# A Conformer block on one core: Strassen products in two more feed-forward chunks, and the last gate blocks in two column pieces

## The chip, the cores and the metric

The kernel runs on one core of one Trainium2 chip. The metric is the device time of one execution in microseconds (us). Times before are the median of three runs; a separate execution was taken by the hardware profiler, and what is read from a trace is of that one. TensorE (PE) multiplies matrices, VectorE (DVE) and ScalarE (ACT) work on elements, GpSimd (POOL) does small things, SyncE (SP) issues DMAs.

## The reference, cut to what matters

Two sequences of 4000 tokens with 512 features go through one block, in bf16:

```python
h = _layernorm(x)
x1 = x + 0.5 * (_silu(h @ w_ff1_a) @ w_ff1_b)        # first feed-forward, 512 -> 2048 -> 512
h = _layernorm(x1)
q, k, v = h @ w_q, h @ w_k, h @ w_v
p = _softmax(jnp.einsum('btd,bsd->bts', q, k) * scale)
x2 = x1 + jnp.einsum('bts,bsd->btd', p, v) @ w_o     # attention over all 4000 tokens
h = _layernorm(x2) @ w_pw1                           # 512 -> 1024
h = h[..., :D] * _sigmoid(h[..., D:])                # the gate
dc = depthwise(h, dw)                                # 3 taps along the tokens
dc = (dc - mu) / jnp.sqrt(var + 1e-05)               # mu, var over all 8000 tokens
x3 = x2 + _silu(dc) @ w_pw2
h = _layernorm(x3)
x4 = x3 + 0.5 * (_silu(h @ w_ff2_a) @ w_ff2_b)       # second feed-forward
return _layernorm(x4)
```

## The kernel before

The 8000 tokens are 16 chunks (NCK), 8 for each sequence: 7 of 512 tokens (CHUNK) and one of 416. A chunk has four token tiles of 128. The kernel works in stages: the first feed-forward, chunk by chunk (`ff1(c)`); attention, with the convolution of earlier chunks beside it; the end of the convolution, which has to wait for the statistics of all tokens; the second feed-forward (`ff2(c)`) with the convolution's last product (`pw2`) of the chunks ahead of it. Nearly every instruction is issued through one helper, so the profile has it on line L93, and groups are told by their tiles. These are memory regions:

- `xt`: token tiles of the residual stream, and in attention forms of queries, keys and values
- `work`: layer-normalized tokens, transposed (`lnT`), small statistics, and sums of the second weight (`st.w`)
- `wff`: the feed-forward's weights (`Wa` for 512 to 2048, in 8 pieces of 256 columns; `Wb` for 2048 to 512), in the convolution `Wp1` and gate values
- `keys`: the hidden activations of a feed-forward chunk, in attention the transposed keys
- `sums`: sums for the Strassen products: of weights (`wsum`), of tokens (`lts`), and a copy of one product (`m5`)
- `s0` to `s3`, `y0` to `y3`: the eight PSUM banks (numbers 0 to 3 and 4 to 7 in the code)

**First product of a feed-forward chunk, plain.** It has 16 blocks f. A block is four matmuls of 512 columns (tokens) into one S bank (`ff_first`), then one Silu on ScalarE into `keys`.

**The same as Strassen.** Four blocks make a quad (`ff_quad`): a product of 2 x 2 halves (features in, features out) with tokens in two halves, by seven products p1 to p7 in place of eight, each of four matmuls of 256 columns. It runs in four steps on the banks 6 (y2), 3 (s3), q % 2 (s0 or s1) and 2 (s2):

- step a: p1 into y2, ScalarE copies it to h (s0 or s1); p5 into s3, ScalarE copies it to `m5`
- step b: p2 onto y2 and its Silu; p6 onto h; VectorE adds h + m5 into s2
- step c: p7 onto h; p3 onto s2 and its Silu; VectorE adds h + m5 into `m5`, and its Silu
- step d: p4 onto h and its Silu

So a quad has two ScalarE copies and two VectorE adds more than four blocks. It needs four sums of weight quarters (`wa_sums`, VectorE, once for a feed-forward; for the second they are made ahead, kept in DRAM and read back by `wa_back`) and four sums of the chunk's normalized tokens (`ln_sums`, VectorE, for each chunk). A list, `self.fast`, says which chunks run as quads: in the first feed-forward chunks 2 to 14, in the second 1 to 14. `ff_ring` says which S banks are left to other work in a chunk.

**Second product.** It is Strassen in all these chunks: units of eight matmuls of 256 columns into y0 and y1 (`ff_units`), which are issued in the next chunk at the blocks named in `ticks`; their sums of activations (`ff_sums`, `keys<-keys 128x1024`) and of weights (`ff_weights`, `work<-wff 128x2048`) are VectorE's.

**Where the second feed-forward starts.** Its chunk 0 follows the convolution's end directly: `pw1` of the last chunk (gate blocks, four matmuls over 416 columns, of which `conv_b` and `conv_a` make two for each quarter of the features), depthwise (`depthwise`, `s<-wff 128x418`), statistics, ScalarE's swishes (`work<-keys,work`), `pw2`, layer norm, transposes on TensorE, and then the first two blocks from two half-chunk products (`self.early`). In chunk 0 `pw2` of chunks 1 and 2 and the swishes of chunks 1, 2 and 3 run beside the blocks.

**What sets the order.** The program text is only a list of operations with their buffers. A planner (`Plan`) puts all of them in order on each engine: it estimates how long each takes and when a DMA has landed, lets TensorE take what is ready within 8 us of the list's order and other engines within 16 us, and runs six passes. Each engine then executes its list strictly in that order. So a changed estimate or an operation more can move instructions anywhere. For a DMA the planner's lines are these:

```python
if n.size:
    begin = max(s + (400 if n.turn else n.dur + 400), pipe)
    pipe = begin + n.size / (180 if n.turn else 260)
    n.land = pipe - s + 1000
```

Here `s` is the time of issue, `pipe` the time at which the bytes issued so far are through, and `n.turn` says that the DMA transposes.

At the very start (`head`) the tokens of chunk 0 come tile by tile; the layer norm of each tile (statistics on VectorE, a power on GpSimd, the normalization on VectorE as `work<-xt,work`), its transposes on TensorE (`y<-work 128x128`) and their copy on ScalarE (`work<-y`) are followed by the tile's 128 columns of the first four blocks (`s<-work,wff 128x128`).

Of the kernel before, what the change touches and what calls it, by code (L numbers as in the profile page):

```python
# [8 lines left out]
ALU = mybir.AluOpType  # L9
# [3 lines left out]
B, T, D, F, KW = 2, 4000, 512, 2048, 3  # L13
# [96 lines left out]
class Plan:  # L110

    PASSES = 6
    SPARE = 3000
    TABLES = {AF.Silu: 1, AF.Exp: 2, AF.Tanh: 2, AF.Sigmoid: 3, AF.Sqrt: 4}
# [158 lines left out]
    def once(self):  # L273
# [43 lines left out]
        while len(order) < len(self.nodes):  # L317
# [238 lines left out]
class Conformer:  # L556
# [35 lines left out]
    def memory(self):  # L592
# [11 lines left out]
        self.b_wsum = [E.buf("wasum", n * 4096, 4096) for n in range(4)]  # L604
# [772 lines left out]
    def wa_sums(self, w, b_w, n):  # L1377

        v = w.rearrange("p (h c) (i k f) -> p h c i k f", h=2, k=2, f=128)
        (a11, a12), (a21, a22) = [[v[:, h, :, :, k, :] for h in range(2)] for k in range(2)]  # L1380
        s1, s2, s3, s4 = self.wsum
        b1, b2, b3, b4 = [[b] for b in self.b_wsum]
        out, x, y, op, rd, wr = ((s1, a21, a22, ALU.add, [], b1), (s2, s1, a11, ALU.subtract, b1, b2),
                                 (s3, a11, a21, ALU.subtract, [], b3), (s4, a12, s2, ALU.subtract, b2, b4))[n]
        for h in range(2):
            self.S.op("DVE", lambda e, h=h: e.tensor_tensor(out=out[:, h], in0=x[:, h], in1=y[:, h], op=op),
                      reads=rd + b_w, writes=wr)
# [22 lines left out]
    def wa_back(self):  # L1410
# [6 lines left out]
                              for half in range(2)], reads=self.b_wsd, writes=self.b_wsum)  # L1417
# [13 lines left out]
    def ff_quad(self, c, q, st):  # L1431
# [9 lines left out]
                 3: (m(3), [self.b_wsum[3]], B(1, 1), right), 4: (w(1, 1), wa, T(3), [self.b_lts[s][3]]),  # L1441
                 5: (m(0), [self.b_wsum[0]], T(0), [self.b_lts[s][0]]),
                 6: (m(1), [self.b_wsum[1]], T(1), [self.b_lts[s][1]]),
                 7: (m(2), [self.b_wsum[2]], T(2), [self.b_lts[s][2]])}
# [68 lines left out]
    def ff_ring(self, c, f):  # L1513
        self.ring = [7] if self.fast[c] else [3, 6, 7] if f < 5 and c and self.fast[c - 1] else [0, 1, 2, 3]

    def ff_chunk(self, c, st, hook, done):

        fast = self.fast[c]
        own = {11: (0, 1), 12: (3,), 15: (2,)} if fast else {9: (0, 1), 10: (2, 3)}
        for f in range(FC):  # L1520
# [3 lines left out]
            if not fast:  # L1524
# [882 lines left out]
    def pw1(self, t, cb, bank=None):  # L2407
        ps, b_ps = bank or self.sbank()
        n, W = TPC if width(t) == CHUNK else TPC - 1, width(t)
        if t == NCK - 1:  # L2410
            moves = [(ps[:, 0:W], self.lin[:, :, 0:W])]
# [5 lines left out]
        for out, x in moves:  # L2417
            for cc in range(DC):
                self.mm(out, self.Wp1[:, cc, cb * 128:(cb + 1) * 128], x[:, cc], cc == 0 and out is moves[0][0], cc == DC - 1,
                        [self.b_Wp1] + self.b_lnT[1 if t == NCK - 1 else 0], b_ps, skip_group_check=True)  # L2420
# [208 lines left out]
    def program(self, any_score):  # L2629
# [50 lines left out]
        def ff1(c):  # L2680
            def hook(f):
# [7 lines left out]
                if c == 1 and f in (4, 5, 6, 7):  # L2689
                    self.wa_sums(self.Wa, self.b_Wa, (0, 1, 3, 2)[f - 4])  # L2690
# [23 lines left out]
        self.fast = [1 < c < NCK - 1 for c in range(NCK)]  # L2714
# [168 lines left out]
        heads = [self.sbank() for _ in all_t]  # L2883
        for cc in range(DC):
            self.swish(1, cc, 0)
# [77 lines left out]
        self.fast = [0 < c < NCK - 1 for c in range(NCK)]  # L2963
# [63 lines left out]
```

## Time and profile before

| what | value |
|---|---|
| median of 3 runs | 1877.64 us (1877.13 to 1879.52) |
| profiled execution | 1879.46 us |
| its span, first to last instruction | 1875.7 us |
| mean granted TensorE clock | 0.998 |
| TensorE busy | 1851.9 us, 99% |
| VectorE busy | 1465.4 us, 78% |
| ScalarE busy | 1309.2 us, 70% |
| GpSimd busy | 134.6 us, 7% |

In lines of the profile an entry gives the start in us, the duration in us, the engine, the operation, the tiles as out<-in with the shape, and a count of instructions that were merged; square brackets give the engine's idle time just before and what ended it. The printed duration of matmuls holds the time until the last result is written, and so overlaps the next one's.

### The profile page before, as it was taken

What the parts mean: (1) busy time and instruction counts of PE and PEld (TensorE: products, weight loads), DVE (VectorE), ACT (ScalarE), POOL (GpSimd) and SP (SyncE); (2) the same over time, 40 slices, a digit from 0 to 9 for tenths busy, and PEclk for the clock granted to TensorE, in tenths of its full rate; (3) what the DMA queues carried; (4) which work ended last, traced back from release to release, by engine and by line L of the source; (5) the groups of instructions that cost most, each with busy time, mean ns of one, the idle gap of its engine ahead of it and who ended that gap; (6) DMA issues with size and microseconds to landing.
All of it is one profiled execution on the core that took longest, in us unless ns stands there. A gap on an engine that the chain in (4) does not pass through costs nothing.

```text
span 1875.7 us, 39058 instructions
## 1 busy us (share of the span) xinstructions
PE 1851.9 (99%) x15271; PEld 1444.6 (77%) x15384; DVE 1465.4 (78%) x3188; ACT 1309.2 (70%) x2421; POOL 134.6 (7%) x302
## 2 busy tenths in 40 slices
PE   9999999999999999999999999999998999999998
PEld 5888888866777777777677777777774888888886
DVE  7888888868768777766777677767778888888885
ACT  5777777744666777667667677777668787777773
POOL 1000000000000000000000001000011000000000
PEclk9999999999999999999999999999999999999999
DMA  8323344197545655447954444444365222212111
GB/s 191 102 79 91 80 112 107 53 266 217 177 143 149 171 163 165 109 131 169 243 141 128 135 122 111 128 133 124 106 206 169 78 57 73 75 46 62 48 43 34
DMA packets 325014, 231.52 MB, mean 123 GB/s; under 512 B 204179, under 2 KB 295638, under 8 KB 324566
## 3 DMA queue, kind: packets, MB, share of 16 engines
q1 hardware_dynamic: 324294, 228.68, 44.6%
q8 instruction: 123, 2.02, 0.4%
q14 instruction: 69, 0.57, 0.1%
q10 hardware_dynamic: 528, 0.26, 0.0%
HBM read 128.44 MB, written 55.79 MB: 98 GB/s over the span
## 4 chain that ended last, share of the span: by engine, by line
PE 95%; ACT 2%; DVE 1%; DMA 1%; issue 1%; POOL 0%; SPq 0%; DVEq 0%; ACTq 0%
PE y L93 48%; PE s L93 47%; DVE work L93 1%; ACT work L93 1%; ACT sums L93 1%; DMA work<-work 0%; DVE xt L93 0%; DMA xt<-in_x_dram 0%; POOL work L93 0%; ACT keys L93 0%; ACT xt L93 0%; DVE s L93 0%; DVE wff L93 0%; ACT wff L93 0%; ACT s L93 0%
## 5 line engine op out<-in xcount | busy, mean ns | idle before, releaser
L93 ACT ACTIVATE sums<-s 128x512 bf16<-128x512 f32 (+2 forms) x494 | 287.0, 584 | 120.5 <-PE s L93 117.7
L93 ACT ACTIVATE keys<-s 128x512 bf16<-128x512 f32 (+2 forms) x284 | 166.3, 588 | 181.4 <-PE s L93 164.7
L93 DVE TENSOR_TENSOR sums<-sums 128x512 bf16<-128x512 bf16 (+3 forms) x528 | 195.8, 398 | 68.9 <-ACT sums L93 64.3
L93 PE MATMUL y<-work,keys 128*128 128x256 bf16 x1920 | 244.7, 273 | 0.0
L93 PE MATMUL s<-work,keys 128*128 128x256 bf16 (+5 forms) x1430 | 219.7, 290 | 1.9 <-ACT sums L93 0.4
L93 ACT ACTIVATE work<-xt,work 128x512 bf16<-128x512 bf16 x268 | 208.2, 785 | 10.3 <-DVE work L93 10.3
L93 PE MATMUL y<-sums,keys 128*128 128x256 bf16 (+1 forms) x1440 | 212.6, 270 | 0.0
L93 PE MATMUL y<-wff,keys 128*128 128x256 bf16 (+2 forms) x1590 | 208.7, 276 | 0.4 <-DVE xt L93 0.4
L93 PEld LDWEIGHTS y<-work,keys 128*128 128x128 bf16 x1920 | 187.9, 98 | 25.0
L93 PE MATMUL s<-sums 128*128 128x256 bf16 x1296 | 194.4, 273 | 0.0
L93 DVE TENSOR_TENSOR keys<-keys 128x1024 bf16<-128x1024 bf16 (+2 forms) x262 | 169.0, 663 | 28.6 <-ACT keys L93 14.8
L93 PE MATMUL y<-work,wff 128*128 128x256 bf16 (+2 forms) x1116 | 188.6, 292 | 0.0
L93 PEld LDWEIGHTS y<-wff,keys 128*128 128x128 bf16 (+1 forms) x1592 | 151.2, 98 | 32.4 <-issue 3.3
L93 DVE BATCH_NORM_STATS2 work<-xt 128x6 f32<-128x512 bf16 x251 | 164.1, 681 | 5.0 <-DMA xt<-in_x_dram 4.2
L93 PEld LDWEIGHTS s<-work,keys 128*128 128x128 bf16 (+1 forms) x1456 | 118.2, 97 | 56.8 <-ACT sums L93 5.1
L93 PEld LDWEIGHTS y<-sums,keys 128*128 128x128 bf16 x1440 | 137.1, 98 | 27.1 <-issue 6.1
L93 POOL TENSOR_TENSOR work<-work 128x4 f32<-128x4 f32 (+3 forms) x107 | 91.0, 851 | 804.2 <-DVE work L93 801.7
L93 PE MATMUL y<-sums,xt 128*128 128x256 bf16 (+1 forms) x960 | 145.6, 270 | 0.0
L93 PE MATMUL s<-work,wff 128*128 128x512 bf16 (+5 forms) x668 | 141.8, 347 | 2.8 <-DVE work L93 2.7
L93 PEld LDWEIGHTS s<-sums 128*128 128x128 bf16 x1296 | 126.7, 98 | 20.0
L93 PE MATMUL s<-work 128*128 128x512 bf16 (+4 forms) x513 | 122.9, 374 | 5.8 <-DVE work L93 1.4
L93 PE MATMUL s<-xt,keys 128*128 128x256 bf16 (+1 forms) x816 | 124.3, 270 | 2.6 <-DVE xt L93 2.3
(143 smaller groups left out, 3182.6 us busy)
## 6 DMA issues: line engine op xcount, KB each, us to landing
xt<-kfd SPq DMA_DIRECT2D x98, 384.0 KB, 3.3
xt<-v12d SPq DMA_DIRECT2D x105, 256.0 KB, 2.8
xd<-xt SPq DMA_DIRECT2D x28, 512.0 KB, 3.0
xt<-xd SPq DMA_DIRECT2D x28, 512.0 KB, 4.6
out_dram<-xt SPq DMA_DIRECT2D x14, 512.0 KB, 3.0
xt<-in_x_dram SPq DMA_DIRECT2D x13, 512.0 KB, 4.0
dcvd<-wff SPq DMA_DIRECT2D x48, 128.0 KB, 2.1
keys<-dcvd SPq DMA_DIRECT2D x12, 512.0 KB, 4.0
```

Of the source, the lines that this page charges most:

```text
L93: return getattr(eng, self.name)(*self.args, **self.kw)
```

## The change

It has five parts.

1. `self.fast` of the first feed-forward begins with chunk 1 instead of 2. The weight sums, until now made in chunk 1 at f = 4 to 7, are made in chunk 0 at f = 8 to 15, in two halves by output features (`part`), with a buffer for each half, so that a half needs four of the eight weight pieces.
2. `self.fast` of the second feed-forward begins with chunk 0, and `self.mixed` is set: chunk 0 has its blocks 0 to 3 plain, and blocks 4 to 15 as three quads. Its token sums are made at f = 0 and 1. For its first four blocks `ff_ring` takes the S banks in an order (`self.turn`) that continues the one of the convolution's end. Its first unit of the second product is no longer issued at the end of chunk 0.
3. `pw1` of the last chunk has the first two of the four `a` and of the four `b` blocks in two column pieces, 256 and 160: the first piece reads token tiles 0 and 1 alone.
4. The planner takes a transposing DMA that stands behind bytes of others to land 1500 ns later (`BEHIND`).
5. The half-chunk products of `self.early` clear their bank once for both halves.

```diff
+    BEHIND = 1500
...
             if n.size:
                 begin = max(s + (400 if n.turn else n.dur + 400), pipe)
+                behind = self.BEHIND if n.turn and pipe > s + 400 else 0
                 pipe = begin + n.size / (180 if n.turn else 260)
-                n.land = pipe - s + 1000
+                n.land = pipe - s + 1000 + behind
...
-    def wa_sums(self, w, b_w, n):
-
-        v = w.rearrange("p (h c) (i k f) -> p h c i k f", h=2, k=2, f=128)
+    def wa_sums(self, w, b_w, n, part):
+
+        at = slice(part * HF // 2, (part + 1) * HF // 2)
+        v = w.rearrange("p (h c) (i k f) -> p h c i k f", h=2, k=2, f=128)[:, :, :, at]
...
+        rd = b_w[part * len(b_w) // 2:(part + 1) * len(b_w) // 2]
...
     def ff_ring(self, c, f):
-        self.ring = [7] if self.fast[c] else [3, 6, 7] if f < 5 and c and self.fast[c - 1] else [0, 1, 2, 3]
+        if c == 0 and self.mixed and f == 2:
+            self.rings["S"] = 0
+        self.ring = (self.turn if self.mixed else [0, 1, 2, 3]) if c == 0 and f < 4 else [7] if self.fast[c] else [3, 6, 7] if f < 5 and c and self.fast[c - 1] else [0, 1, 2, 3]
...
-            if not fast:
+            if not fast or mixed and q == 0:
                 self.ff_block(c, f, st)
             elif r == 0:
                 quad = self.ff_quad(c, q, st)
...
+            if mixed and f < 2:
+                self.ln_sums(c, f)
...
     def pw1(self, t, cb, bank=None):
         ps, b_ps = bank or self.sbank()
+        first = cb % DC < 2
...
         if t == NCK - 1:
-            moves = [(ps[:, 0:W], self.lin[:, :, 0:W])]
+            b_x, cut = self.b_lnT[1], [0, 2 * TILE, W] if first else [0, W]
+            moves = [(ps[:, lo:hi], self.lin[:, :, lo:hi]) for lo, hi in zip(cut, cut[1:])]
...
-        for out, x in moves:
+        for n, (out, x) in enumerate(moves):
+            rd = b_x[2 * n:2 * n + 2] if t == NCK - 1 and first else b_x
...
-                if c == 1 and f in (4, 5, 6, 7):
-                    self.wa_sums(self.Wa, self.b_Wa, (0, 1, 3, 2)[f - 4])
+                if c == 0 and f >= 8:
+                    self.wa_sums(self.Wa, self.b_Wa, (0, 1, 3, 2)[f % 4], (f - 8) // 4)
...
-        self.fast = [1 < c < NCK - 1 for c in range(NCK)]
+        self.fast = [0 < c < NCK - 1 for c in range(NCK)]
+        self.mixed = False
...
+        self.turn = [self.b_S.index(b) for _, b in heads[2:] + heads[:2]]
...
-                            cc == 0, cc == DC - 1, [self.b_Wa[f * self.NWA // FC]] + self.b_lnT[0][2 * h:2 * h + 2], b_ps)
+                            cc == 0 and h == 0, cc == DC - 1, [self.b_Wa[f * self.NWA // FC]] + self.b_lnT[0][2 * h:2 * h + 2],
+                            b_ps, skip_group_check=True)
...
-        self.fast = [0 < c < NCK - 1 for c in range(NCK)]
+        self.fast, self.mixed = [c < NCK - 1 for c in range(NCK)], True
```

More of the change, by code (lines that the diff above doesn't have):

```diff
@@ L603, in memory @@
         self.wsum = [E.view(n * 4096, 2048).rearrange("p (c i f) -> p c i f", c=2, i=HF) for n in range(4)]
-        self.b_wsum = [E.buf("wasum", n * 4096, 4096) for n in range(4)]
+        self.b_wsum = [[E.bufs("wasum", [(n * 4096 + c * 2048 + k * 1024, 1024) for c in range(2)]) for k in range(2)]
+                       for n in range(4)]
         self.lts = [[E.view(16384 + s * 4096 + n * 1024, 512).rearrange("p (t c k) -> p t c k", t=2, c=2)
@@ L1416, in wa_back @@
                                                                self.wsd[half].rearrange("p (m f) -> p m f", m=8))
-                              for half in range(2)], reads=self.b_wsd, writes=self.b_wsum)
+                              for half in range(2)], reads=self.b_wsd, writes=sum(self.b_wsum, []))
     def ln_sums(self, c, step):
@@ L2416, in pw1 @@
                 moves.append((ps[:, n * TILE:W], self.lnT[0][:, n, :, tile_rows(t, n)]))
[L2417 removed]
+        for n, (out, x) in enumerate(moves):
+            rd = b_x[2 * n:2 * n + 2] if t == NCK - 1 and first else b_x
             for cc in range(DC):
[L2419 to L2420 removed]
+                self.mm(out, self.Wp1[:, cc, cb * 128:(cb + 1) * 128], x[:, cc], cc == 0 and n == 0, cc == DC - 1,
+                        [self.b_Wp1] + rd, b_ps, skip_group_check=True)
         return ps, b_ps
```

21 lines of the change are left out of this document (11 added, 10 removed).

## The prediction

> **What bounds the kernel now.** I read the page first: the span, the busy shares and the chain that ended last.
>
> ```profile
> span 1875.7 us, 39058 instructions
> PE 1851.9 (99%) x15271; PEld 1444.6 (77%) x15384; DVE 1465.4 (78%) x3188; ACT 1309.2 (70%) x2421; POOL 134.6 (7%) x302
> PE 95%; ACT 2%; DVE 1%; DMA 1%; issue 1%; POOL 0%; SPq 0%; DVEq 0%; ACTq 0%
> ```
>
> TensorE (PE) is busy for 99% of the span and carries 95% of the chain. So a change can act in two ways only: fewer columns through TensorE, or another length of the few stalls between them. The profiled execution took 1879.46 us, 3.76 more than its span; the median of the three runs is 1877.64. I work out a difference from the trace and take it off that median; off the profiled time it would give a figure 1.8 higher.
>
> The order of the instructions of the changed program shows where they went; it gives no time. TensorE has 100 matmuls more: 12 for each of seven quads (four in the first feed-forward's chunk 1, three in the second's chunk 0) and 16 for the split gate blocks. There are 14 more ScalarE copies and 14 more VectorE adds of quads, 8 more token sums on VectorE, and no more DMAs.
>
> **1. Columns saved.** The timeline of TensorE gives the price of a matmul as it is paid in a full queue, which is the distance of starts and not the printed duration (that holds the pipeline's tail).
>
> ```profile
> 200.33 1.91 PE L93 MATMUL y<-work,keys 128*128 128x256 bf16 x16
> ...
> 209.93 0.60 PE L93 MATMUL s<-sums 128*128 128x256 bf16 x4
> ...
> 1436.17 3.62 PE L93 MATMUL s<-work,wff 128*128 128x512 bf16 x16
> 1439.62 1.03 PE L93 MATMUL s<-work 128*128 128x512 bf16 x4
> ```
>
> Between the first two rows 88 matmuls of 256 columns start in 9.60 us: 0.109 each. Sixteen of 512 columns take 3.45 us: 0.2156 each. Four plain blocks are sixteen of the latter, 3.45 us; a quad is 28 of the former, 3.06. That saves 0.395, and 2.77 us for seven. The split of four gate blocks adds 16 instructions and no columns; two of 256 cost 0.218 against 0.2156 for one of 512, so 0.003 each, 0.04 together. Both lie on TensorE, which is the path.
>
> **2. The head of the kernel.** The weight sums of the first feed-forward now run on VectorE in chunk 0. Nobody needs them soon, but the planner puts four of them (512 elements each) ahead of the normalization of token tile 3, and the first of the four waits for the DMAs of weight pieces 0 to 3. VectorE works in order, so that normalization waits too, and behind it TensorE's transposes of tile 3, ScalarE's copy of them, and the last column piece of the first four blocks.
>
> ```profile
> 2.59 3.83 SPq L93 DMA_DIRECT2D wff<-in_w_ff_a_dram  x5
> wff<-in_w_ff_a_dram SPq DMA_DIRECT2D x5, 256.0 KB, 5.6
> 9.05 0.41 DVE L93 TENSOR_SCALAR work<-xt,work 128x512 bf16<-128x512 bf16 x1 [0.52 <-POOL work L93]
> 12.44 2.47 DVE L93 BATCH_NORM_STATS2 work<-xt 128x6 f32<-128x512 bf16 x4 [2.98 <-DMA xt<-in_x_dram]
> 47.23 0.76 DVE L93 TENSOR_TENSOR sums<-work 128x512 bf16<-128x512 bf16 x2 [0.95 <-DMA work<-work]
> 47.91 0.88 DVE L93 TENSOR_TENSOR sums<-work,sums 128x512 bf16<-128x512 bf16 x2
> 9.91 0.39 PE L93 MATMUL y<-work 128*128 128x128 bf16 x4
> 10.32 10.00 PE L93 MATMUL s<-work,wff 128*128 128x128 bf16 x68
> 11.65 3.26 ACT L93 ACTIVATE keys<-s 128x512 bf16<-128x512 f32 x6 [0.71 <-PE s L93]
> ```
>
> Piece 3 is the third of SyncE's five issues, at about 3.6 to 4.1, and lands a median 5.6 later: 9.2 to 9.7, take 9.3 (the tokens of chunk 1, behind it in the queue, are there by 12.44). The four sums at 0.38 to 0.44 each end at 10.9, the normalization at 11.3 instead of 9.46. The transposes then start at 11.35 instead of 9.91, and take 0.4 to their end; the copy takes 0.6, so 12.35. Four matmuls of 128 columns and their tail (0.4) close the first block, and its Silu starts at 12.75 instead of 11.65: 1.1 late. The fifth block needs the bank that this Silu empties, and from there on TensorE had no gap in which to catch up. I take **+1.0**; the bounds are 0.3 (the weights are there by 8.5) and 1.5.
>
> Further on, VectorE is full in just the stretch that has to make the token sums for chunk 1's first quads:
>
> ```profile
> 20.00:44.00 24.00, 23.89 (x158) 14.83 (x159) 23.18 (x41) 14.56 (x28) 1.40 (x1) 1.00 0.62 139
> ```
>
> (Columns: length, busy PE, weight load, VectorE, ScalarE, GpSimd, clock, DMA.) Following VectorE's new order with these durations from 16.5 on, the token sums of tiles end at 23.9 and 25.4, while TensorE reaches the products that need them at 25.9 and 27.7; the first quad's add ends at 29.2, its user comes at 30.7. So no stall, with 1.5 to 2 us in hand; if that cover is gone it costs what the four quads saved, 1.6.
>
> **3. Gate blocks of the last chunk in two pieces.** The timeline before the convolution's last chunk:
>
> ```profile
> 1406.37 0.39 PE L93 MATMUL y<-work 128*128 128x128 bf16 x4
> 1407.79 0.86 PE L93 MATMUL s<-work,wff 128*128 128x416 bf16 x4 [1.04 <-DVE work L93]
> ...
> 1417.17 0.69 PE L93 MATMUL s<-wff 128*128 128x418 bf16 x3
> 1417.91 0.38 PE L93 MATMUL y<-work 128*128 128x512 bf16 x1
> ```
>
> TensorE ends its transposes at 1406.6 (four of 0.056) and begins the first gate block at 1407.79, when the copies of token tiles 2 and 3 are done: 1.2 us empty. The new order has twelve matmuls of 256 columns there, from three blocks, that need tiles 0 and 1 alone: 1.31 us of work that fits the hole. From 1407.79 to 1417.9 TensorE ran without a gap, so what comes earlier stays earlier, unless VectorE, at work almost without a break on the convolution's statistics, holds it. **−1.1**, bounds −1.25 and 0.
>
> **4. Second feed-forward, chunk 0.** Its 22 us:
>
> ```profile
> 1427.60:1449.60 22.00, 20.83 (x103) 10.56 (x106) 18.73 (x34) 19.28 (x33) 1.88 (x1) 0.92 0.55 156
> 1439.10 1.88 POOL L93 TENSOR_TENSOR work<-work 128x4 f32<-128x4 f32 x1 [12.07 <-DVE work L93]
> 1445.46 0.81 PE L93 MATMUL s<-work 128*128 128x512 bf16 x3 [0.50 <-ACT keys L93]
> L93 ACT ACTIVATE s<-y 128x512 f32<-128x512 f32 x56 | 32.9, 588 | 0.6
> L93 ACT ACTIVATE work<-keys,work 128x512 bf16<-128x512 bf16 x40 | 31.6, 812 | 8.1 <-PE y L93 7.8 <-PE s L93 0.3
> L93 DVE TENSOR_TENSOR s<-s,sums 128x512 f32<-128x512 f32 x56 | 38.8, 694 | 2.8 <-PE s L93 2.3 <-ACT keys L93 0.3 <-ACT xt L93 0.3
> ```
>
> Three quads bring 6 copies of 0.59 to ScalarE (3.5 us), 6 adds of 0.69 and 4 token sums of 0.4 to VectorE (5.7). ScalarE has 2.7 free and VectorE 3.3, so some work has to move out: the swishes (0.81 each) and the feed-forward's own sums can go on into chunk 1, and TensorE gets second-matmul units of chunk 0 as filling. Along the new order TensorE is 0.5 to 1 us behind ScalarE at each bank. At one place VectorE is late: the shift behind GpSimd's 1.88 us power is now ahead of a 1.2 us weight sum and of the second quad's add, and TensorE, which wants that add, waits 1.0. Against that the 0.50 wait at 1445.46 goes. Net **+0.5**; bounds −0.6 and, if nothing moves out, +3.
>
> **5. Transposes behind other DMAs.** The planner now takes a DMA transpose queued behind another transfer to land 1.5 us later. The place:
>
> ```profile
> 835.66 2.75 SPq L93 DMA_TRANSPOSE work<-work  x2
> 841.85 0.42 ACT L93 ACTIVATE work<-work 128x256 bf16<-128x256 bf16 x1 [3.46 <-DMA work<-work]
> 841.86 0.60 PE L93 MATMUL y<-sums,keys 128*128 128x256 bf16 x4
> 844.30 0.53 PE L93 MATMUL s<-xt,keys 128*128 128x208 bf16 x4 [1.84 <-DVE xt L93]
> ```
>
> ScalarE stands 3.46 us at transposes, VectorE's reciprocal behind ScalarE, and TensorE loses 1.84. In the new order ScalarE's instructions at this place are the same, but the transposes go ahead of one 1.2 us transpose of keys and one of the casts before them is ScalarE's. I take **−0.7**, between 0 and −2.0, nearer to the half because the queue of the same engine stays. Other neighbours moved by a place or two along all of attention, where waits on DMAs are far shorter.
>
> **Sum.** −2.77 + 0.04 + 1.0 − 1.1 + 0.5 − 0.7 = −3.0 us: 1877.64 becomes **1874.6** (a span of 1872.7). That is −0.16%, within the 0.2% (3.75 us) that a measurement of this kernel can tell from no change.
>
> **The clock.** Around the second feed-forward's start the granted clock falls:
>
> ```profile
> 1426.00:1430.00 4.00, 2.56 (x20) 1.94 (x20) 3.37 (x11) 3.36 (x7) 0.70 (x1) 0.78 1.09 357
> 1430.00:1432.00 2.00, 1.62 (x9) 1.21 (x10) 1.90 (x4) 1.74 (x3) 0.00 (x0) 0.59 1.07 378
> ```
>
> Together these make about 3.4 us at half clock. I leave the term at zero, since the same sparse stretch is in the new order; bounds are −0.8 (it goes) and +1.7 (a second one of full matmul work, half of 3.4). [...]
>
> **Rivals.**
> - *Both waits close* (18%). The transposes land before ScalarE needs them (−2.0 instead of −0.7), and chunk 0 covers its hand-offs and loses its old wait (−0.6 instead of +0.5): −5.4, 1872.2. For it: the transposes have one queue place less ahead. Against: ScalarE's order is unchanged there.
> - *A second slow stretch of the clock* (10%), if the second feed-forward's quads leave TensorE with more short gaps: −3.0 + 1.7 = −1.3, 1876.3.
> - *VectorE becomes the bound in the first feed-forward* (8%), 23.18 of 24 us being full: the four quads' 1.6 is not kept: −1.4, 1876.2.
> - *Slower: the three quads run in series* (8%). A quad is four hand-offs: 4 × 0.44 of products, two of 0.59 to ScalarE, two of 0.69 to VectorE and four tails of 0.16, 5.0 us. With one 0.81 swish ahead at each of ScalarE's two, 6.6, or 3.5 over the 3.06 of its own matmuls, 10.6 for three; the convolution's twenty matmuls of 512 columns cover 4.3 of it at most, some 3 since they wait for VectorE too. Then +7.6 stands in place of +0.5: +4.1, 1881.7. It decides where ScalarE's queue is over 1 us late at the first quad's copy. For it: 19.28 of 22 us busy. Against: along the new order the copies come in time.
>
> **The numbers.** The forecast has 56%, with a range of its own of 1873.0 to 1876.2. Faster by over 0.2% is a third of it and the first rival, 36%; slower by over 0.2% is three quarters of the last, 6%; within, 58%. The range leaves out the last rival and the ends of the first: 1871.8 to 1878.2.
>
> **What would show it.** Right: 28 matmuls of 256 columns in place of 16 of 512 for each quad, at 0.109; the first Silu at about 12.7; the gap before the last chunk's first gate block under 0.2; one wait of about 1 us on VectorE in the second feed-forward's chunk 0; the wait at 844 about halved. Wrong: a Silu at 11.7, ScalarE waits of over 2 us in the quads, a wait on VectorE between 25 and 45, or new waits in attention.

## The result, and the profile after

The changed kernel takes 1875.51 us (median of 22 executions, 1873.52 to 1877.11), the kernel before 1878.69 (22 executions beside it, 1876.68 to 1880.54). The ratio is 0.9982 with a 95% interval of 0.9976 to 0.9988: 3.2 us or 0.17% faster, where 3.0 was forecast. The profiled execution took 1876.08 us.

From the page of the changed kernel, the span, the busy line and the chain:

```profile
span 1871.9 us, 39333 instructions
PE 1851.6 (99%) x15370; PEld 1453.3 (78%) x15484; DVE 1471.1 (79%) x3212; ACT 1317.5 (70%) x2441; POOL 135.4 (7%) x302
PE 93%; DVE 2%; ACT 2%; DMA 1%; issue 1%; SPq 1%; DVEq 0%
```

Busy time is no measure of what changed (1851.6 against 1851.9): a printed duration runs on past the next start (3.62 us for sixteen matmuls of 512 columns whose starts take 3.45), and there are 99 matmuls more. What counts is when the same instruction starts. In a part of the program where both orders issue the same things, the difference of the starts says how far the changed kernel is ahead by then. The timeline of TensorE gives these anchors, after:

```profile
199.64 1.91 PE L93 MATMUL y<-work,keys 128*128 128x256 bf16 x16
...
842.41 0.60 PE L93 MATMUL y<-sums,keys 128*128 128x256 bf16 x4
842.85 0.52 PE L93 MATMUL s<-xt,keys 128*128 128x208 bf16 x4
...
1403.93 0.39 PE L93 MATMUL y<-work 128*128 128x128 bf16 x4
1404.15 1.75 PE L93 MATMUL s<-work,wff 128*128 128x256 bf16 x16
...
1422.05 0.40 PE L93 MATMUL s<-work 128*128 128x128 bf16 x4 [1.25 <-ACT work L93]
...
1485.50 0.60 PE L93 MATMUL s<-sums,wff 128*128 128x256 bf16 x4
```

and two rows of before beside those that the prediction shows:

```profile
1425.57 0.40 PE L93 MATMUL s<-work 128*128 128x128 bf16 x4 [1.25 <-ACT work L93]
...
1488.85 0.60 PE L93 MATMUL s<-sums,wff 128*128 128x256 bf16 x4
```

| stretch | before | after | ahead | gained in the stretch | forecast |
|---|---|---|---|---|---|
| head and first feed-forward (`y<-work,keys` x16) | 200.33 | 199.64 | 0.69 | 0.7 | 0.6 (1.6 columns, -1.0 head) |
| attention (by 1350 us) | | | 2.32 | 1.6 | 0.7 |
| to the second feed-forward's transposes (`s<-work` 128x128) | 1425.57 | 1422.05 | 3.52 | 1.2 | 1.1 |
| second feed-forward, chunk 0 and start of 1 (`s<-sums,wff`) | 1488.85 | 1485.50 | 3.35 | -0.2 | 0.7 (1.2 columns, -0.5 waits) |

The figure at 1350 us is the median over matmuls of the same tiles. So two parts came out near the forecast, and two did not: attention gained 0.9 more, the second feed-forward 0.9 less. These two misses cancel. TensorE's last matmul ends 3.2 earlier; the spans differ by 3.7, the last 0.5 of it in what follows that matmul, which nothing in the change touches.

The head, in the timeline after:

```profile
9.00 1.10 DVE L93 TENSOR_TENSOR sums<-wff 128x512 bf16<-128x512 bf16 x3 [0.75 <-DMA wff<-in_w_ff_a_dram]
...
10.47 0.41 DVE L93 TENSOR_SCALAR work<-xt,work 128x512 bf16<-128x512 bf16 x1
...
11.12 0.39 PE L93 MATMUL y<-work 128*128 128x128 bf16 x4
...
12.63 3.19 ACT L93 ACTIVATE keys<-s 128x512 bf16<-128x512 f32 x6 [0.49 <-PE s L93]
```

The first sums wait for the weights until 9.00, the normalization of tile 3 comes behind four of them at 10.47, its transposes at 11.12, the first Silu at 12.63 instead of 11.65. That is the chain of the prediction, link by link.

VectorE's window in the first feed-forward (length, PE, weight load, VectorE, ScalarE, GpSimd, clock, DMA) did not become a bound:

```profile
20.00:44.00 24.00, 23.89 (x195) 18.46 (x196) 22.46 (x45) 16.09 (x32) 1.09 (x1) 1.00 0.62 151
```

### The profile page after: what moved, and what is told of

Read it like the earlier page. It is cut to its first block, busy times and chain, and to the rows that moved or that the text cites. A ratio compares the mean times of both kernels' runs of the same rounds, so it can differ in the third digit from the quotient of the medians.

```text
span 1871.9 us, 39333 instructions
## 1 busy us (share of the span) xinstructions
PE 1851.6 (99%) x15370; PEld 1453.3 (78%) x15484; DVE 1471.1 (79%) x3212; ACT 1317.5 (70%) x2441; POOL 135.4 (7%) x302
## 4 chain that ended last, share of the span: by engine, by line
PE 93%; DVE 2%; ACT 2%; DMA 1%; issue 1%; SPq 1%; DVEq 0%
PE y L93 48%; PE s L93 45%; ACT sums L93 1%; DVE work L93 1%; DVE xt L93 1%; SPq L93 1%; ACT work L93 0%; DMA kfd<-xt 0%; DVE sums L93 0%; DMA vhd<-wff 0%; DVE wff L93 0%; ACT wff L93 0%; ACT keys L93 0%; DMA wff<-keysd 0%; DMA work<-work 0%
## 5 line engine op out<-in xcount | busy, mean ns | idle before, releaser
L93 ACT ACTIVATE sums<-s 128x512 bf16<-128x512 f32 (+3 forms) x501 | 290.4, 584 | 112.2 <-PE s L93 108.4
L93 ACT ACTIVATE keys<-s 128x512 bf16<-128x512 f32 (+2 forms) x271 | 158.7, 588 | 176.0 <-PE s L93 158.1
L93 PE MATMUL s<-sums 128*128 128x256 bf16 x1380 | 206.1, 273 | 0.8 <-DVE sums L93 0.6
L93 PE MATMUL y<-work,wff 128*128 128x256 bf16 (+3 forms) x1168 | 196.1, 291 | 0.0
L93 PEld LDWEIGHTS s<-sums 128*128 128x128 bf16 x1380 | 134.6, 98 | 23.9 <-DVE sums L93 0.8
L93 PEld LDWEIGHTS y<-work,wff 128*128 128x128 bf16 x1168 | 113.0, 98 | 25.8 <-ACT s L93 0.4
L93 PE MATMUL s<-work 128*128 128x512 bf16 (+5 forms) x494 | 118.7, 376 | 5.3 <-DVE work L93 1.4
```

What stands on the lines that cost most here:

```text
L93: return getattr(eng, self.name)(*self.args, **self.kw)
```

## The experiments

All start from the changed kernel unless said otherwise, and each was timed in 11 executions beside 33 of the kernel before. They came in three groups, with medians of the kernel before of 1878.65 (n_behind0 to n_pw1), 1879.84 (the next four in the table) and 1878.83 (the last four), so the ratios are to be compared rather than the medians. The last four columns give, for the profiled execution, how far the kernel is ahead of the one before at four places (300 us; 1350 us; the first transposes of the second feed-forward; 1530 us), all from the timeline of TensorE.

| kernel | edit | median, us | ratio to before (95%) | 300 | 1350 | transposes | 1530 |
|---|---|---|---|---|---|---|---|
| changed kernel | | 1875.51 | 0.9982 (0.9976 to 0.9988) | 0.68 | 2.32 | 3.52 | 3.35 |
| n_behind0 | planner's term 0 | 1874.78 | 0.9979 (0.9970 to 0.9988) | 0.59 | 2.25 | 2.90 | 4.15 |
| n_ff1 | first feed-forward as before | 1876.55 | 0.9990 (0.9981 to 0.9999) | -0.14 | 1.51 | 2.14 | 3.13 |
| n_ff2 | second's chunk 0 plain | 1875.89 | 0.9983 (0.9974 to 0.9992) | -0.97 | 0.85 | 2.05 | 2.05 |
| n_pw1 | gate blocks whole | 1877.95 | 0.9994 (0.9985 to 1.0003) | -0.13 | 1.94 | 1.65 | 3.43 |
| p_pw1 | kernel before, gate blocks split | 1877.53 | 0.9987 (0.9978 to 0.9996) | 0.06 | 0.43 | 1.89 | 1.83 |
| e_wsum | weight sums after all pieces | 1877.72 | 0.9989 (0.9980 to 0.9998) | -0.59 | 2.16 | 3.02 | 2.11 |
| e_wsum_b0 | the same, planner's term 0 | 1879.61 | 1.0000 (0.9991 to 1.0009) | -2.41 | -0.72 | 0.64 | 0.14 |
| e_2quads | two quads, not three | 1876.78 | 0.9984 (0.9975 to 0.9993) | 0.42 | 1.93 | 3.13 | 3.78 |
| h5 | weight sums behind tile 3 | 1875.58 | 0.9983 (0.9974 to 0.9992) | 0.96 | 2.69 | 4.13 | 3.34 |
| l1 | earlier layer norm of chunk 1 | 1878.48 | 0.9996 (0.9987 to 1.0005) | 0.39 | 1.99 | 3.19 | 3.18 |
| h5l1 | both | 1875.81 | 0.9983 (0.9974 to 0.9992) | 1.06 | 2.44 | 3.88 | 3.93 |
| h5l1b0 | both, planner's term 0 | 1878.28 | 0.9997 (0.9988 to 1.0006) | 0.84 | 2.27 | 3.55 | 2.36 |

An interval is some 3.4 us wide, as much as the whole effect. So the medians tell little about a single part; the places in the traces tell more, though one execution still differs from the next. One such difference has a name: a stretch of half clock at the start of the second feed-forward, worth 1.24 us (last section), stands in the profiled executions of the kernel before, the changed kernel, n_ff2, p_pw1, e_wsum, h5 and h5l1b0, and in none of the other seven. In the last column those seven are ahead by about 1.24 for the clock alone, an estimate from one pair of traces.

A gap of TensorE is here the distance of two starts less what the first matmul takes in a full queue (0.056 us for 128 columns, 0.109 for 256, 0.2156 for 512); the idle time that a row prints in brackets is some 0.16 shorter, because the printed duration runs on by as much (3.62 us where the starts take 3.45).

**The planner's term for transposes, and attention.** Two kernels undo one possible cause each.

```diff
 n_behind0:
-    BEHIND = 1500
+    BEHIND = 0
```

> The changed kernel with the planner's term for transposes set back to 0; all else stays. Theory A (the term itself shortens attention, by what the two traces differ between 425 and 1400 us, 1.6): the time goes up by 1.6 against the changed kernel, to 1.5 below the kernel before, and TensorE's wait near 844 us (1.84 in the kernel before) is back. The prediction's size of the same theory: up by 0.7. Theory B (any replanning moves attention's short waits by chance, the term has no effect of its own): the wait near 844 need not come back, others appear elsewhere, and the change against the changed kernel is anywhere between -1.5 and +1.5.

```diff
 n_ff1:
-        self.fast = [0 < c < NCK - 1 for c in range(NCK)]
+        self.fast = [1 < c < NCK - 1 for c in range(NCK)]
...
-                if c == 0 and f >= 8:
-                    self.wa_sums(self.Wa, self.b_Wa, (0, 1, 3, 2)[f % 4], (f - 8) // 4)
+                if c == 1 and f in (4, 5, 6, 7):
+                    for part in range(2):
+                        self.wa_sums(self.Wa, self.b_Wa, (0, 1, 3, 2)[f - 4], part)
```

> The changed kernel with the first feed-forward as it was: chunk 1 in plain blocks, the weight sums in chunk 1 at f = 4 to 7. Theory A: at 300 us this kernel is 0.68 behind the changed one (1.58 of columns come back, 0.90 of the head goes), the first Silu starts at 11.65 in place of 12.63, and attention, which keeps the planner's term, stays 1.6 shorter than before. Theory B: attention's order is planned anew here too, so its length differs from the changed kernel's by up to 1.5 either way. Rival for the head: if tile 3's tokens and not the weight sums made the first Silu late, it stays near 12.6 and 1.58 is lost in full.

With the term at 0 the wait near 844 us stayed away. The timeline of TensorE in n_behind0, at the place where the kernel before waits 1.84:

```profile
841.31 0.60 PE L93 MATMUL y<-sums,keys 128*128 128x256 bf16 x4
841.75 0.52 PE L93 MATMUL s<-xt,keys 128*128 128x208 bf16 x4
```

Between 300 and 1350 us n_behind0 gains 1.66 and n_ff1 1.65, the changed kernel 1.64. So the term is not needed for what attention gained; nor are the quads of chunk 1. Nor did the time of n_behind0 go up by 0.7 or 1.6 as theory A has it: its median is 0.7 below the changed kernel's. A third kernel shows that the wait belongs to the old order and is no accident of one execution:

```diff
 p_pw1: the kernel before, with the function pw1 of the changed kernel
```

> The kernel before with the column pieces of the last chunk's gate blocks alone; its order in attention is that of the kernel before, instruction for instruction. Theory: the wait near 844 us follows from that order, so it is there again with 1.5 to 2 us, and attention is as long as before; the hole ahead of the first gate block is gone, and the time is 1.1 below the kernel before. Rival: the wait near 844 was one execution's late transfer; then it is missing here, and this profiled span is some 3 below the one of before.

Its order in attention is that of the kernel before, and the wait is back in the timeline:

```profile
838.42 2.42 SPq L93 DMA_TRANSPOSE keys<-keysd  x1
...
841.76 0.42 ACT L93 ACTIVATE work<-work 128x256 bf16<-128x256 bf16 x1 [3.42 <-DMA work<-work]
...
844.22 0.53 PE L93 MATMUL s<-xt,keys 128*128 128x208 bf16 x4 [1.79 <-DVE xt L93]
```

Against that the changed kernel, whose order here leaves two transposes and a follower of half the length:

```profile
835.70 2.51 SPq L93 DMA_TRANSPOSE work<-work  x2
838.25 1.27 SPq L93 DMA_TRANSPOSE keys<-keysd  x1
...
839.52 0.42 ACT L93 ACTIVATE work<-work 128x256 bf16<-128x256 bf16 x1 [0.58 <-DMA work<-work]
```

ScalarE waits 3.42 in the one and 0.58 in the other, though the transposes of `work` start at nearly the same time (835.66 in the kernel before, 835.70 here). What differs in the queue is the transpose of `keys` behind them, 2.42 against 1.27, and that another one of `keys` goes ahead of them in the old order (834.32 in the kernel before). That order of the four transposes does not decide it alone: e_wsum and e_wsum_b0 have the same four in the same order, with 1.25 and 1.28 for the last, and there ScalarE waits 2.05 and 1.67 and TensorE not at all. Why the DMAs took longer in the old order was not tried. All twelve kernels whose order in attention is another gain 1.4 to 2.8 between 300 and 1350 us, three of them with the term at 0 (1.66, 1.69, 1.43). They have seven different orders between them: n_ff2, n_pw1, e_2quads and l1 have that of the changed kernel, and h5l1 that of h5. p_pw1, with the order of the kernel before, gains 0.37. So theory A, and with it the prediction's cause, falls as far as the term is not needed: the old order had one bad place, and each new one that was tried passes it. Theory B's statement that the term has no effect of its own fits this but is not shown, since the term alone was not put into the kernel before; its expectation that gains and losses are evenly spread did not come true.

New waits came too, and they follow from the order in part: the gap after 602 us is 0.34 in the changed kernel, 0.64 in n_ff2, 0.45 in n_pw1 and 0.62 in l1, all four with the same order there; the one after 591 is 0.50, 0.26, below 0.24 and 0.40. In the changed kernel a transfer stands ahead of both: ScalarE waits 1.94 us for `work<-work` until 589.04, and VectorE 1.07 for `wff<-keysd` until 600.39. Whether their landing makes the sizes differ was not tried.

**The head.** n_ff1, without weight sums in chunk 0, has its first Silu at 11.79: its rival is out. Its length at 300 us, -0.14, is as expected (0.68 behind was expected against the changed kernel, 0.82 came). The delay is larger than 1.0 in other executions of the same order. VectorE's wait and the first Silu in n_pw1:

```profile
9.95 1.10 DVE L93 TENSOR_TENSOR sums<-wff 128x512 bf16<-128x512 bf16 x3 [0.76 <-DMA wff<-in_w_ff_a_dram]
...
13.40 3.19 ACT L93 ACTIVATE keys<-s 128x512 bf16<-128x512 f32 x6 [0.49 <-PE s L93]
```

The first sums start at 9.00, 9.49, 9.95, 9.44 and 9.46 in the five kernels with this order (changed, n_ff2, n_pw1, e_2quads, l1), and the first Silu at 12.63, 12.95, 13.40, 12.89 and 12.92: the head costs 1.0 to 1.75 by when the weights land.

```diff
 e_wsum:
-        rd = b_w[part * len(b_w) // 2:(part + 1) * len(b_w) // 2]
+        rd = b_w
```

> The changed kernel with both halves of the weight sums of the first feed-forward reading all eight weight pieces, so that none of them can stand ahead of token tile 3's normalization. Theory (the head's delay is VectorE waiting for the first weight pieces, 1.0 to 1.75 by how late these land in an execution): the first Silu starts at 11.6 to 11.8, and at 300 us the kernel is 1.58 ahead of the kernel before; the time is 1.0 to 1.7 below the changed kernel's. Rival: VectorE, 22.5 of 24 us busy between 20 and 44 us, now has some 2.8 us more of sums there, the token sums and adds of chunk 1's quads come late, and TensorE loses between 25 and 45 us what the head gains: no change.

The head came back in full (chunk 1's transposes start within 0.02 of the kernel before), and yet at 300 us the kernel is 0.59 behind instead of 1.58 ahead. The windows of VectorE and the waits of TensorE in e_wsum:

```profile
20.00:44.00 24.00, 23.90 (x196) 18.55 (x197) 23.80 (x51) 16.43 (x32) 1.09 (x1) 1.00 0.62 154
44.00:68.00 24.00, 22.57 (x190) 17.70 (x190) 19.82 (x47) 19.50 (x36) 2.02 (x2) 1.00 0.38 84
```

```profile
56.28 0.81 ACT L93 ACTIVATE work<-xt,work 128x512 bf16<-128x512 bf16 x1 [1.63 <-DVE work L93]
...
61.03 0.61 PE L93 MATMUL y<-work,wff 128*128 128x256 bf16 x4 [0.66 <-ACT keys L93]
...
67.06 1.05 PE L93 MATMUL y<-wff,keys 128*128 128x256 bf16 x8 [0.32 <-DVE keys L93]
```

VectorE is busy for 23.80 of 24 us, where the changed kernel has 22.46, and TensorE for 22.57 of 24 in the stretch after it, with four gaps (0.42, 0.31, 0.82, 0.49). The first row shows the way: ScalarE stands 1.63 for what VectorE has to make before a chunk can be normalized, and then has these normalizations between the Silus that TensorE waits for. The rival is right, some 20 us later than it said. So the early weight sums pay about 1 us at the head to save 2 between 53 and 67 us, and the prediction's third rival (VectorE as the bound) is real and close: with 1.3 us more of VectorE work in those 24 us it came true.

```diff
 e_wsum_b0: as e_wsum, and BEHIND = 0
```

> As e_wsum, and the planner's term for transposes is 0. If what shortened attention is any new order and not the term, the wait near 844 us stays away here too, attention is 1.5 to 2 shorter than before, and the second feed-forward begins without a slow stretch of the clock as it did with the term at 0 alone: 5 to 5.5 below the kernel before, the fastest so far. If the orders differ by chance, between 3 and 5 below.

The wait near 844 stayed away, and attention gained 1.69, as the first half says. The rest missed: 0.2 below the kernel before, not 5. It has the waits of e_wsum, one single gap of 1.28 at 165.5 us that its neighbours lack (the same kind stands in n_ff2 at 164 us, with 1.32, where VectorE waited 2.22 for transposed tokens), and gaps of 2.09 and 0.86 at the start of the second feed-forward's chunk 1. There the first token sum starts 3.2 us after the row of the four DMA transposes ends (1445.33 and 1448.52), in the changed kernel 1.3 (1444.89 and 1446.22); why they land so late was not tried.

```diff
 h5:
-        rd = b_w[part * len(b_w) // 2:(part + 1) * len(b_w) // 2]
+        rd = b_w[part * len(b_w) // 2:5 if part == 0 else len(b_w)]
```

> The changed kernel with the first half of the weight sums reading five weight pieces in place of four. The planner then puts the normalization of token tile 3 ahead of them and keeps them early, so VectorE does not carry them into the stretch from 45 to 68 us as in e_wsum. Theory (the loss at the head is that one normalization standing behind the sums; the loss in e_wsum was VectorE's load after it): first Silu at 11.7 to 11.9, no new waits up to 100 us, at 300 us 1.4 to 1.6 ahead of the kernel before where the changed kernel was 0.68; time 0.9 to 1.6 below the changed kernel's. Rival: the sums, now later by a piece, hold chunk 1's statistics and norms, and a wait of 0.5 or more appears between 20 and 70 us: half the gain or none.

The timeline of h5:

```profile
9.45 0.41 DVE L93 TENSOR_SCALAR work<-xt,work 128x512 bf16<-128x512 bf16 x1 [0.74 <-POOL work L93]
11.25 1.43 DVE L93 TENSOR_TENSOR sums<-wff 128x512 bf16<-128x512 bf16 x4 [1.38 <-DMA wff<-in_w_ff_a_dram]
...
12.24 3.26 ACT L93 ACTIVATE keys<-s 128x512 bf16<-128x512 f32 x6 [0.49 <-PE s L93]
```

The normalization of tile 3 is ahead of the sums now (9.45), no new wait appears up to 100 us, and the first Silu starts at 12.24. That is half of the way: the planner also moved the transposes behind more of the first blocks. At 300 us h5 is 0.96 ahead, h5l1 1.06; the five executions of the changed kernel's order had 0.68, -0.13, 0.42, 0.39 and 0.36 (n_ff2, before its single gap), 0.34 in the mean. So 0.6 to 0.7 is gained at the head, where 0.9 to 1.6 was expected; the median, 1875.58, is that of the changed kernel.

**The gate blocks in two pieces.**

```diff
 n_pw1:
-        first = cb % DC < 2
+        first = False
```

> The changed kernel with all gate blocks of the last chunk in one column piece. Theory: the hole of 1.2 us between the transposes of the last chunk's tokens and its first gate block is back, the stretch from there to the second feed-forward is 1.08 longer, and the time 1.1 longer than the changed kernel's, 2.1 below the kernel before. Rival: VectorE's statistics set the end of that stretch anyway, so only part, 0 to 0.5, is lost. The waits near 591 and 844 us are as in the changed kernel if they follow from the order.

The timelines, without the pieces (n_pw1) and with them (p_pw1):

```profile
1404.72 0.39 PE L93 MATMUL y<-work 128*128 128x128 bf16 x4
1406.15 0.86 PE L93 MATMUL s<-work,wff 128*128 128x416 bf16 x4 [1.04 <-DVE work L93]
```

```profile
1405.56 0.39 PE L93 MATMUL y<-work 128*128 128x128 bf16 x4
1405.79 1.75 PE L93 MATMUL s<-work,wff 128*128 128x256 bf16 x16
```

The hole of 1.2 us is back in the one and gone in the other. From 1350 us to the transposes p_pw1 gains 1.46 on the kernel before, and n_pw1 loses 0.29 where the changed kernel gains 1.20: 1.5 by both, more than the hole, because gaps of 0.41 and 0.29 among the transposes ahead of it went with it. By the ratios the pieces are worth 0.12% (n_pw1) and 0.13% (p_pw1), 2.3 to 2.4 us; the rival is out, the rest above 1.5 lies within the intervals.

**Second feed-forward, chunk 0.**

```diff
 n_ff2:
-        self.fast, self.mixed = [c < NCK - 1 for c in range(NCK)], True
+        self.fast, self.mixed = [0 < c < NCK - 1 for c in range(NCK)], False
```

> The changed kernel with the second feed-forward's chunk 0 in plain blocks throughout; the order of everything ahead of it is the same. By the trace of the changed kernel the three quads save 1.19 in columns and bring about 1.3 of new waits (copies, VectorE's adds, VectorE at the transposes of chunk 1's tokens): between 0.3 faster and 0.2 slower than the changed kernel. By the prediction's size (0.5 of waits): 0.7 slower. The wait near 591 us (0.5) is there and the one near 844 is not, if these follow from the order of the instructions; if they are chance of one execution, they differ.

It is 0.4 slower than the changed kernel by the medians, between the two expectations and closer than the intervals can tell. By the traces it neither gains nor loses from the transposes to 1530 us (2.05 and 2.05), where the changed kernel loses 0.17. The waits that ate the columns are these in the changed kernel:

```profile
1434.38 0.61 PE L93 MATMUL s<-sums 128*128 128x256 bf16 x4 [0.19 <-ACT sums L93]
...
1446.70 1.22 PE L93 MATMUL s<-sums 128*128 128x256 bf16 x8 [0.56 <-DVE sums L93]
...
1446.22 0.43 DVE L93 TENSOR_TENSOR sums<-work 128x512 bf16<-128x512 bf16 x1 [1.45 <-DMA work<-work]
...
1438.95 5.94 SPq L93 DMA_TRANSPOSE work<-work  x4
```

The first (a gap of 0.35) is a copy of ScalarE that comes late; one of 0.26 follows at 1439; the largest, 0.72, is the first quad of chunk 1, whose token sums wait for four DMA transposes in series (1438.95 to 1444.89, landed by 1446.2). VectorE stands for 1.45 there.

```diff
 e_2quads:
-            if not fast or mixed and q == 0:
+            if not fast or mixed and q < 2:
...
-        self.ring = (self.turn if self.mixed else [0, 1, 2, 3]) if c == 0 and f < 4 else [7] if self.fast[c] else ...
+        self.ring = (self.turn if self.mixed else [0, 1, 2, 3]) if c == 0 and f < 8 else [7] if self.fast[c] else ...
```

> The changed kernel with two quads in place of three in the second feed-forward's chunk 0 (blocks 0 to 7 plain). If each quad keeps its 0.395 and the waits there come from the number of hand-offs, one quad less costs 0.4 of columns and takes a third or more of the 1.36 of waits away: between 0.1 slower and 0.5 faster than the changed kernel. If the waits come from VectorE standing at chunk 1's transposes, they stay, and it is 0.4 slower.

With one quad less the wait at chunk 1's transposes shrank to 0.27, but others came (gaps of 0.39, 0.45 and 0.60):

```profile
1432.15 2.76 PE L93 MATMUL s<-work,wff 128*128 128x512 bf16 x12 [0.22 <-DVE xt L93]
...
1436.94 1.05 PE L93 MATMUL y<-work,keys 128*128 128x256 bf16 x8 [0.29 <-DVE keys L93]
...
1448.08 0.81 PE L93 MATMUL y<-work 128*128 128x512 bf16 x3 [0.44 <-DVE xt L93]
```

Its ratio, 0.9984, is that of the changed kernel within the interval. What it gains in this stretch, 0.65, is less than the clock alone makes (1.24, last section). So the waits come neither from the number of quads alone nor from the transposes alone.

```diff
 l1:
-                if c == 0 and f in (2, 4):
-                    ti = 1 + f // 2
+                if c == 0 and f in (1, 2):
+                    ti = 1 + f
...
-                        self.ln_job(1, "in", "ACT", (3, 4, 5, 7, 7, 8, 8, 8, 9, 9))
+                        self.ln_job(1, "in", "ACT", (2, 3, 3, 4, 4, 4, 5, 5, 5, 5))
```

> The changed kernel with the convolution's last product for tiles 2 and 3 of chunk 1 at f = 1 and 2 in place of 2 and 4, and chunk 1's layer norm listed 1 to 4 blocks earlier, in the second feed-forward's chunk 0. Theory (the wait of 0.7 to 2 at the start of chunk 1 is the chain residual, statistics, norm, four transposes in series, token sum; it is late because the quads brought TensorE forward): the transposes end some 2 us earlier than in the changed kernel, that wait goes, and the kernel is 0.5 to 0.8 below the changed one. Rival: ScalarE, 20.0 of 22 us busy there, is the limit; then the copies of the quads come later by the swishes that the earlier product needs, waits of the same size appear inside chunk 0, and the time stays.

The window of 22 us in l1, and its timeline:

```profile
1424.09:1446.09 22.00, 20.11 (x147) 13.44 (x148) 21.83 (x45) 21.52 (x37) 1.01 (x1) 1.00 0.59 170
```

```profile
1433.95 0.60 PE L93 MATMUL y<-work,wff 128*128 128x256 bf16 x4 [0.34 <-ACT keys L93]
...
1440.78 1.04 PE L93 MATMUL y<-work 128*128 128x512 bf16 x4 [0.42 <-DVE xt L93]
...
1447.33 0.61 PE L93 MATMUL s<-sums 128*128 128x256 bf16 x4 [0.35 <-DVE s L93]
...
1436.94 5.14 SPq L93 DMA_TRANSPOSE work<-work  x4
```

The transposes end 2.8 earlier (1442.08 against 1444.89), as planned. But VectorE is busy for 21.83 of 22 us and ScalarE for 21.52 (19.30 and 20.02 in the changed kernel's same window), and the waits are now at ScalarE's and VectorE's hand-offs inside the chunk; the one at chunk 1's start (a gap of 0.52) is VectorE's add. The time stays, as the rival said: both engines are full, and what is moved forward pushes something else back. Being full is not enough for a wait, though: n_pw1 has 21.27 and 21.65 of 22 us there (from 1426 us) and is the best of all, with waits of 0.39 and 0.28 only. Over all kernels with three quads, this stretch (transposes to 1530 us) gains between -1.2 and -0.2 where the clock is slow and between -0.5 and 1.8 where it is not. With the 1.24 (from one pair of traces) taken off the latter, eight of these ten traces lose time here against the kernel before, up to 1.7, and the best gains 0.5, where n_ff2 without any quad has 0.00. So the traces do not show that the three quads pay; the 0.4 by which the median of n_ff2 is slower lies within the intervals. The waits of the quads are a matter of the order, and none of the edits tried commands them.

```diff
 h5l1: the edits of h5 and l1;  h5l1b0: and BEHIND = 0
```

> Both edits, of h5 and of l1. If they are independent, the sum of the two: 1.4 to 2.4 below the changed kernel, 4.6 to 5.6 below the kernel before.

> As h5l1, with the planner's term for transposes at 0. If the term does nothing of its own for attention, the wait near 844 us stays away, attention is 1.5 to 2 shorter than in the kernel before, and the time is within 0.7 of h5l1. If it does, this kernel is 1.6 above h5l1.

h5l1 is as fast as the changed kernel and no faster: h5's 0.6 is there, l1's gain is not. In h5l1b0 the wait near 844 stays away and attention is as short (1.43 against 1.38), as expected of a term without effect there; but its time, 2.5 above h5l1, misses the 0.7. In the trace it falls back behind the second feed-forward's transposes (3.55 down to 2.36), but these 1.2 are as much as the half clock made in the one pair of traces (1.24), and it stands in this execution and not in that of h5l1. So the trace does not explain the medians' 2.5, and what does is open. No run beat the changed kernel beyond its interval; n_behind0, with the term at 0, is as fast.

## Why the prediction was right, and where it was not

The sum was right, -3.0 forecast and -3.2 measured, in part because two errors of 0.9 cancelled.

1. *Columns saved* (-2.77). At 300 us the changed kernel is 0.68 ahead after losing 0.90 at the head (chunk 1's transposes start at 21.06, before at 20.16): 1.58, which is four times 0.395. For the three quads of the second feed-forward it can't be separated from their waits.
2. *The head* (+1.0). Mechanism and chain as described. In the profiled execution 0.90; over five executions of this order the first Silu is 1.0 to 1.75 late, above the bound of 1.5 in one. The step that was too low is the landing of the weights (9.3 taken; the sums began at 9.0 to 9.95). The cover that VectorE was to have in chunk 1 held, and e_wsum, with 1.3 us more of VectorE's work from 20 to 44 us, shows that there was not much more of it.
3. *Gate blocks in two pieces* (-1.1, bounds -1.25 and 0). The hole is gone as described. The stretch gained 1.5, outside the bound: the gaps among the transposes ahead of the hole were not counted.
4. *Second feed-forward, chunk 0* (+0.5, bounds -0.6 and +3). This term was mis-sized: from the transposes to 1530 us the kernel lost 0.17 where the columns save 1.19, so waits cost 1.36 more than before. (The gaps account for 1.1 of it: 0.35, 0.26 and 0.72, some 0.45 in gaps of 0.03 to 0.16 at hand-offs, less the old 0.66; the rest is in no single gap.) The place named, VectorE's add behind GpSimd's power and a weight sum, is there, but with 0.26 and not 1.0. The old wait at 1445.46 went. What was missing is the start of chunk 1, 0.72, whose tokens' transposes are no longer hidden when TensorE arrives 1.2 us sooner, and ScalarE's late copy, 0.35. The prediction looked at the hand-offs of the quads and not at what the next chunk needs in time. With the columns of term 1 the three quads were to gain 0.7; at the same clock only n_pw1's trace shows a gain (0.5).
5. *Transposes behind other DMAs* (-0.7, between 0 and -2.0). The wait went altogether (842.41 and 842.85 follow without a break), and attention gained 1.6, new waits of 0.84 at 591 and 602 included, which were among the prediction's signs of being wrong. The forecast was half of what came, and the cause was wrong in that the term is not needed: with it at 0 the same happens. That this term of the sum had the right sign is luck.
6. *The clock* (0). One stretch before, one after, each of 3.4 us at half clock; right for these two executions. That the sparse stretch brings the slow one was the author's estimate: e_2quads has the same idle times there and stays at 1.00.

Of the rivals, the first (both waits close) was half true: the wait at 844 closed, the hand-offs did not. VectorE as the bound of the first feed-forward was one edit away. A second slow stretch and the quads in series did not come: no ScalarE wait in the quads is over 2 us.

## What to carry to other kernels

Where an order is planned, a changed estimate or an operation more gives a new order everywhere; before a gain far from the edit is put down to the edit, undo the edit and see whether the gain goes. Work taken off the critical engine brings forward the time at which the next stage's inputs are due: the longest serial chain into that stage (here residual, statistics, normalization, four transposes, sum) belongs in the forecast. And early work on a second engine has a price on both sides: look at how full that engine is in the stretch that it would otherwise fall into. Last, before two traces are compared stretch by stretch, see whether the clock is the same in both (here a stretch at half made 1.24 us).

## What was not expected of the hardware

The half clock at the start of the second feed-forward is there in 7 of the 14 profiled executions; in the other 7 the clock stays at 1.00. In the changed kernel it reads 0.50 from 1423.6 to 1426.9 us, in the kernel before 0.50 from 1428.3 to 1431.6, and in each of the two the granted clock falls short by 1.7 us in all, which is a stretch of 3.4 us at half. The waits around it need not differ. The changed kernel and e_2quads issue the same instructions there, after the same waits; first the changed kernel's timeline and window, then those of e_2quads:

```profile
1424.09 1.86 PE L93 MATMUL s<-work,wff 128*128 128x256 bf16 x8 [1.02 <-DVE work L93]
1425.75 1.06 PE L93 MATMUL s<-work 128*128 128x128 bf16 x8
1427.42 0.81 PE L93 MATMUL s<-work,wff 128*128 128x256 bf16 x6 [0.61 <-DVE work L93]
```

```profile
1424.00:1428.00 4.00, 3.30 (x22) 2.50 (x23) 2.71 (x8) 2.89 (x6) 0.00 (x0) 0.63 0.93 299
```

```profile
1422.44 0.40 PE L93 MATMUL s<-work 128*128 128x128 bf16 x4 [1.25 <-ACT work L93]
...
1426.57 1.68 PE L93 MATMUL s<-work,wff 128*128 128x256 bf16 x11 [0.61 <-DVE work L93]
```

```profile
1424.00:1428.00 4.00, 2.91 (x27) 2.33 (x28) 3.86 (x11) 3.93 (x9) 0.00 (x0) 1.00 1.09 382
```

From the transposes (1422.05 and 1422.44) to the same block (1427.42 and 1426.57) it is 5.37 us with the slow stretch and 4.13 without: 1.24 us. The idle times ahead are the same, 1.25, 0.24 and 1.02 us in the changed kernel and 1.25, 0.24 and 1.01 in e_2quads, and the clock fell in the one and not in the other. So these idle times do not decide it by themselves; what does was not shown.

In whole executions the changed kernel took 1874.43 us (median of 12) where its mean granted clock reads 1.000 and 1876.04 (of 9) where it reads 0.999. That difference of one and the same program is half of what the change gained. The reading is coarse, though: the clock also reads 0.50 at the end of the span (from 1870.7 us on in the changed kernel and from 1872.0 in the kernel before, behind the last matmul), five of the seven profiled executions without the slow stretch read 0.999 too, and in n_ff2 the difference is 0.3 (1875.82 in 6 at 1.000, 1876.11 in 5 at 0.998). How much of the 1.6 us is the slow stretch's stays open.
